# Attention with a gated feed-forward unit: norms in bfloat16, the shift of the scores turned in the bank of the last maxima, tail outputs turned in fp16 parts, and a list schedule that knows when GpSimd holds SBUF

## The chip, the cores and the metric

The kernel runs on one core of a Trainium2 chip. The metric is the device time of an execution in microseconds, given as the median of several runs. The engines are named as in the profile: PE is TensorE's matmuls, PEld its weight loads, DVE is VectorE, ACT is ScalarE, POOL is GpSimd, and SP is the engine that issues all DMAs here.

## The reference

Attention over 8 batches of 8 heads: 576 pooled queries against 1152 keys of 64 dimensions. Its output goes through a feed-forward unit with a gate that mixes the sequence.

```python
q_pool = q.reshape(B, H, S // 2, 2, D).mean(axis=3)
scores = scale * np.matmul(q_pool, k.transpose(0, 1, 3, 2))
scores = scores - np.max(scores, axis=-1, keepdims=True)
attn = np.exp(scores)
attn = attn / (np.sum(attn, axis=-1, keepdims=True) + 1e-09)
x = np.matmul(attn, v)          # heads put side by side: (8, 576, 512)
...
h = np.maximum(x @ w_in, 0.0)   # 512 -> 1024
u, v = h[..., :512], h[..., 512:]
v_n = (v - mean(v)) / np.sqrt(var(v) + 1e-06)
v_s = np.einsum('ts,bsd->btd', w_spatial, v_n) + b_spatial[None, :, None]
out = (u * v_s) @ w_out
```

## The kernel before

All operands are fp32 in memory. Matmuls run in fp16 on parts: a number is scaled by a power of two and written as a head (rounded to fp16) and a rest (what the rounding left), and products are summed over three combinations. `head` is an ACT copy with a scale, `rest` a DVE instruction of three operands, out = in * scale - head, over two tensors that mostly lie in SBUF.

**Attention** goes over 32 pairs of heads. Of the 576 queries of a head, 512 are the main part and 64 the tail; the tails of both heads share tiles. For each pair there are these steps:

- `prep` loads queries and keys, takes their sums of squares on ACT, and calls `scales`: a matmul with a matrix of ones (`ones`, L345) adds a column over all partitions, and three DVE instructions make a power of two from the exponent. This matmul is called the norm. Weights, values and the gated products have norms too. Heads and rests then go to `xq`, `klo` and others.
- `maxima` computes scores roughly, in 27 tiles of 128 queries by 384 keys, each in a PSUM bank (L617 and L608), from which DVE takes the maximum (`mt`, L623). Banks come from a pool of two (`pm`), and from a second pool of two (`pw`) while no unit of the feed-forward part is under way.
- `shift` comes after 15 of the 27 tiles and again at the end. It reduces 5 or 4 columns of maxima (`mx`, L635), turns them on PE by a matmul with the identity into a bank of its own (L639), scales them there, and writes head and rest to `mr` (L642 to L646). Two DMAs bring `mr` into two rows of `xq`, so that the score matmul subtracts the maximum itself.
- `attention` computes scores in two matmuls (L800 and L801, in banks `pss`), exponentials on ACT (L806, into one of eight buffers `pt`), and splits each into two 16-bit halves on POOL (L826). `values` multiplies them with the values (L714, L720, L725) into a bank `o`, of which there is one; when 9 tiles of a head are done, DVE divides (`den`, L693 and L694, then `xm`, L733).
- `tail_values` (L772 to L774) does the same for the tails, and DVE scales its two blocks of 64 by 64 into `xt` (L778). After the fourth pair of a batch, `turn_main` turns the four `xt` on PE by a matmul with `ident2` (L757), and `x_split` makes head (ACT) and rest (DVE) of the result.

**The feed-forward part** runs in four units of two batches each, on PE beside the attention of the following pairs; the last unit runs after the end of attention. It makes the second half of h (L883), its mean and variance, the normalised tiles on DVE (L919 and L925), the first half (L947), the spatial product (L988 and L989), the gated product and its head and rest (L372), and the output (L1031). The three weights are loaded, decoded from 64-bit numbers on DVE and ACT, and split during the first eight pairs.

**The order.** The loops only write down what is to be done. `Order.pin` then lists the instructions: at each step it takes, over all engines, the one that can start first by a table of costs, where on an engine the earliest written of the ready ones goes first, and fixes each engine's order. An engine executes its instructions in that order. The planner keeps `held`, the time for which the last POOL instruction holds the port to SBUF that POOL shares with DVE. A DVE instruction that reads only SBUF (`shared`) and was chosen within that time is put at its end less 130 ns.

Of the kernel before, what the change touches and what calls it, by code (L numbers as in the profile page):

```python
# [31 lines left out]
class Order:  # L32
# [150 lines left out]
    def pin(self, tc):  # L183
# [32 lines left out]
        for _ in prog:  # L216
            best = None
            for e, ns in ready.items():
                if ns:

                    at = {n: max(due[n], wire - 1000) if n in load else due[n] for n in ns}
                    t = max(free[e], min(at.values()))
                    n = min(n for n in ns if at[n] <= t)
                    if best is None or t < best[0]:
                        best = (t, e, n)
# [36 lines left out]
def attn_sgu_kernel(ctx: ExitStack, tc: tile.TileContext, qT, kT, v, w_in, w_spT, b_sp, w_out, out):  # L262
# [41 lines left out]
    ones = const.tile([P, P], F32, name="ones")  # L304
    nc.vector.memset(ones, 1.0)

    ident2 = const.tile([P, D], F32, name="ident2")
# [7 lines left out]
    xt = const.tile([P, NHP, P], F32, name="xt")  # L315
# [24 lines left out]
    def scales(sq, name, up=0):  # L340
# [4 lines left out]
        nc.tensor.matmul(pt[:, :n], lhsT=ones, rhs=sq, start=True, stop=True)  # L345
# [248 lines left out]
    def maxima(i):  # L594
# [5 lines left out]
        for t in range(NT):  # L600
# [25 lines left out]
            if t == 4:  # L626
                yield from shift(st, mt, 0, 5)
        yield
        yield from shift(st, mt, 5, NT)

    def shift(st, mt, a, z):
        X = st["X"]
        n = z - a
        mx = sm.tile([P, NT], F32, name="mx", bufs=2)
        nc.vector.reduce_max(out=mx[:, :n], in_=mt[:, a:z], axis=AX.X)  # L635
        yield
        yield
        pt = ps_m.tile([P, 512], F32, name="pm")
        nc.tensor.transpose(out=pt[:n, :P], in_=mx[:, :n], identity=ident)  # L639
        mr = sm.tile([NT, 2, P], F16, name="mr", bufs=2)  # L640
        m = pt[:n, :P]
        nc.vector.tensor_scalar(  # L642
            out=m, in0=m, scalar1=st["lnp"][:n], scalar2=1.0 / MROW, op0=ALU.subtract, op1=ALU.mult
        )
        nc.vector.tensor_copy(out=mr[:n, 0], in_=m)
        nc.vector.tensor_sub(mr[:n, 1], m, mr[:n, 0])  # L646
        for r in range(2):
            rows = X[D + r : D + r + 1].rearrange("p h s -> p (h s)")
            nc.sync.dma_start(out=rows[:, a * P : z * P], in_=mr[:n, r])
# [90 lines left out]
    def turn_main(i):  # L740
# [13 lines left out]
        if hp == NHP - 1:  # L754
            ps = ps_m.tile([P, 512], F32, name="pm")
            for k in range(NHP):
                nc.tensor.matmul(ps[:, k * D : (k + 1) * D], lhsT=xt[:, k], rhs=ident2, start=True, stop=True)  # L757
            t0 = MAIN + e * TAIL
            x_split(n, slice(0, NHP), slice(t0, t0 + TAIL), ps[:, : NHP * TAIL].rearrange("p (k t) -> p k t", t=TAIL))
# [3 lines left out]
    def tail_values(i):  # L763
# [12 lines left out]
        for h in range(2):  # L776
            rows = slice(h * D, (h + 1) * D)
            nc.vector.tensor_scalar_mul(xt[rows, hp, rows], o[rows, h, 0:D], r[rows])  # L778
# [412 lines left out]
```

## Time and profile before

| | us |
|---|---|
| median of 3 runs | 1218.47 (1217.81 to 1222.07) |
| profiled execution, its time | 1221.1 |
| its span, first to last instruction | 1219.0 |

| stage, us from the start | PE | DVE | ACT | POOL | PE clock |
|---|---|---|---|---|---|
| 0 to 33: first pair's loads and maxima | 11.77 | 20.34 | 16.12 | 7.58 | 0.89 |
| 33 to 290: eight pairs, weights | 215.12 | 231.54 | 197.47 | 218.53 | 0.92 |
| 290 to 1219: 24 pairs, four units | 916.36 | 645.13 | 676.97 | 683.49 | 1.00 |

The second table gives how long each engine was busy. A DVE or POOL instruction that waits for the shared port counts as busy while it waits. Durations of matmuls overlap, since they are pipelined: what one costs PE is the distance from its start to the start of the next.

### The profile page before, as it was taken

What the parts mean: (1) busy time and instruction counts of PE and PEld (TensorE: products, weight loads), DVE (VectorE), ACT (ScalarE), POOL (GpSimd) and SP (SyncE); (2) the same over time, 40 slices, a digit from 0 to 9 for tenths busy, and PEclk for the clock granted to TensorE, in tenths of its full rate; (3) what the DMA queues carried; (4) which work ended last, traced back from release to release, by engine and by line L of the source; (5) the groups of instructions that cost most, each with busy time, mean ns of one, the idle gap of its engine ahead of it and who ended that gap; (6) DMA issues with size and microseconds to landing.
All of it is one profiled execution on the core that took longest, in us unless ns stands there. A gap on an engine that the chain in (4) does not pass through costs nothing.

```text
span 1219.0 us, 34011 instructions
## 1 busy us (share of the span) xinstructions
PE 1143.2 (94%) x13504; PEld 712.6 (58%) x13504; DVE 897.0 (74%) x2163; ACT 890.6 (73%) x1659; POOL 909.6 (75%) x774
## 2 busy tenths in 40 slices
PE   3888888879999999999999999999999999999998
PEld 1555555556666666666666666666665666665453
DVE  5699999997889676865679777865669866841644
ACT  4788778678977887878777887878776786754423
POOL 2769998699888897888787887888887787874000
PEclk9989899899999999999999999999999999999999
DMA  5456464346443553266433443256343421121002
GB/s 189 162 169 169 118 196 120 112 126 169 122 123 95 122 142 105 49 167 179 117 80 99 140 118 89 63 145 196 93 115 98 106 76 47 39 53 45 1 1 78
DMA packets 97151, 135.09 MB, mean 111 GB/s; under 512 B 48544, under 2 KB 56736, under 8 KB 96480
## 3 DMA queue, kind: packets, MB, share of 16 engines
q1 hardware_dynamic: 96992, 132.92, 39.7%
q8 instruction: 106, 1.74, 0.6%
q14 instruction: 53, 0.43, 0.1%
HBM read 81.20 MB, written 9.44 MB: 74 GB/s over the span
## 4 chain that ended last, share of the span: by engine, by line
PE 72%; DVE 16%; ACT 3%; issue 1%; DMA 0%; ACTq 0%; DVEq 0%
PE pss L800 8%; PE pss L801 8%; PE pm L617 7%; PE pw L988 7%; PE pw L883 6%; DVE mt L623 6%; PE pw L1031 5%; PE pw L947 5%; PE o L725 4%; PE o L714 4%; PE o L720 4%; DVE vv L372 2%; PE pss L883 1%; PE pss L988 1%; PE pss L1031 1%
## 5 line engine op out<-in xcount | busy, mean ns | idle before, releaser
L826 POOL TENSOR_TENSOR pt<-pt 128x512 f16<-128x512 f32 x576 | 643.0, 1136 | 154.5 <-ACT pt L806 152.7
L806 ACT ACTIVATE pt<-pss,esc 128x512 f32<-128x512 f32 x576 | 386.7, 686 | 166.3 <-PE pss L801 104.0
L623 DVE TENSOR_REDUCE mt<-pm 128x1 f32<-128x384 f32 x733 | 387.9, 549 | 75.2 <-PE pm L617 66.4
L800 PE MATMUL pss<-qhi,khi 128*128 128x512 f16 x576 | 221.3, 385 | 18.3 <-ACT pt L806 16.9
L801 PE MATMUL pss<-xq,klo 66*128 66x512 f16 x576 | 221.3, 387 | 0.7 <-DMA xq<-mr 0.5
L617 PE MATMUL pm<-khi,qhi 128*128 128x384 f16 x655 | 208.6, 332 | 10.4 <-DVE mt L623 5.2
L714 PE MATMUL o<-vp,pt 128*128 128x65 f16 x2304 | 171.0, 194 | 0.4
L725 PE MATMUL o<-vp,pt 128*128 128x65 f16 x2304 | 169.7, 194 | 0.6 <-POOL pt L826 0.5
L714 PEld LDWEIGHTS <-pt 128*128 128x128 bf16 x2304 | 130.1, 99 | 67.1 <-issue 5.0
L720 PE MATMUL o<-vp,pt 128*128 128x64 f16 x2304 | 168.7, 194 | 0.0
L725 PEld LDWEIGHTS <-pt 128*128 128x128 f16 x2304 | 124.0, 99 | 32.0 <-issue 4.5
L617 PEld LDWEIGHTS <-qhi 128*128 128x128 f16 x768 | 75.3, 100 | 76.5 <-issue 30.2
L720 PEld LDWEIGHTS <-pt 128*128 128x128 bf16 x2304 | 112.2, 99 | 3.3 <-issue 0.3
L883 PE MATMUL pw<-wi_h,xg 128*128 128x512 f16 x240 | 88.4, 378 | 0.0
L801 PEld LDWEIGHTS <-klo 66*128 66x128 f16 x576 | 56.6, 99 | 51.8 <-issue 27.3
L826 POOL TENSOR_TENSOR ptl<-ptl 128x1152 f16<-128x1152 f32 x32 | 74.3, 2321 | 14.4 <-ACT ptl L822 14.4
L947 PE MATMUL pw<-xg,wi_h 128*128 128x512 f16 (+1 forms) x336 | 83.4, 325 | 0.0
L822 ACT ACTIVATE ptl<-pss,esc 128x256 f32<-128x256 f32 (+1 forms) x128 | 63.7, 497 | 26.4 <-PE pss L817 26.2
L988 PE MATMUL pw<-ws_h,vv 128*128 128x512 f16 x216 | 80.6, 379 | 0.0
L1031 PE MATMUL pw<-wo_h,vv 128*128 128x512 f16 x216 | 79.0, 378 | 1.1 <-DVE vv L372 0.9
L623 DVE TENSOR_REDUCE mt<-pw 128x1 f32<-128x384 f32 x131 | 69.6, 543 | 9.3 <-PE pw L617 8.9
L800 PEld LDWEIGHTS <-khi 128*128 128x128 f16 x576 | 57.0, 99 | 26.2 <-issue 6.8
(195 smaller groups left out, 2432.0 us busy)
## 6 DMA issues: line engine op xcount, KB each, us to landing
vt<-in_v_dram SPq DMA_DIRECT2D x56, 576.0 KB
qt<-in_qT_dram SPq DMA_DIRECT2D x32, 576.0 KB
kt<-in_kT_dram SPq DMA_DIRECT2D x32, 576.0 KB
khi<-kn SPq DMA_DIRECT2D x128, 144.0 KB
out_dram<-row SPq DMA_DIRECT2D x24, 256.0 KB
qhi<-xq SPq DMA_DIRECT2D x64, 72.0 KB
klo<-klo SPq DMA_DIRECT2D x32, 144.0 KB
vv<-in_w_in_dram SPq DMA_DIRECT2D x4, 1024.0 KB
```

Source lines behind the costliest of these rows:

```text
L617: nc.tensor.matmul(pm[:, :W], lhsT=qhl[:, h, c0 : c0 + P], rhs=khh[:, h, n * NB : (n + 1) * NB, :], start=True, stop=True,)
L623: nc.vector.reduce_max(out=mt[:, t, n : n + 1], in_=pm[:, :W], axis=AX.X)
L714: nc.tensor.matmul(o[:, t], lhsT=top[:, cols], rhs=vp[:, D : D + D1], start=c == 0 and t == 0, stop=False, skip_group_check=True,)
L720: nc.tensor.matmul(o[:, t, 0:D], lhsT=top[:, cols], rhs=vp[:, 0:D], start=False, stop=False, skip_group_check=True)
L725: nc.tensor.matmul(o[:, t], lhsT=rst[:, cols], rhs=vp[:, D : D + D1], start=False, stop=c == NC - 1, skip_group_check=True,)
L800: nc.tensor.matmul(o, lhsT=khh[:, h, c, :], rhs=qhl[:, h, q], start=True, stop=False)
L801: nc.tensor.matmul(o, lhsT=KL[0:KR, h, c, :], rhs=X[0:KR, h, q], start=False, stop=True)
L806: nc.scalar.activation(pt, ps, AF.Exp, bias=0.0, scale=esc)
L826: nc.gpsimd.tensor_sub(t.bitcast(F16)[..., 0::2], t, t.bitcast(BF16)[..., 1::2])
L883: nc.tensor.matmul(ph, lhsT=xa[:, cc, c0 : c0 + P], rhs=wa[:, cc, DH:DF], start=n == 0, stop=n == 3 * NCC - 1,)
L988: nc.tensor.matmul(pv, lhsT=l, rhs=r[:, 0:MAIN], **fl)
L1031: nc.tensor.matmul(py, lhsT=ga[:, fc, c0 : c0 + P], rhs=wa[:, fc, :], start=m == 0, stop=m == end - 1)
```

## The change

1. **Norms.** `ones` becomes bfloat16, and the sums enter by the upper 16 bits of each fp32 number. A norm is one bfloat16 matmul instead of fp32.
2. **Shift.** The reduced maxima no longer go to SBUF, but into free columns of the bank that held the last tile of maxima (`pm` or `pw`). They are scaled there, and head and rest go to one tile `mc` side by side. One fp16 transpose with a new fp16 identity turns both, into the end of the same bank, and one DVE copy takes them to `mr`. No other bank is taken. The DMAs are the same in number and size.
3. **Tail outputs.** `tail_values` writes head (ACT) and rest (DVE) in fp16 to `xt`, which is doubled. `turn_main` turns the eight parts with an fp16 `ident2`, and one ACT copy takes them; `x_split` is no longer called there.
4. **List schedule.** Where DVE chooses its next instruction, one that reads only SBUF and could start only while POOL holds the port counts as ready at the end of that time less 130 ns. Another instruction can so be chosen ahead of it. Before, it was chosen and then put there.

```diff
@@ Order.pin
                     at = {n: max(due[n], wire - 1000) if n in load else due[n] for n in ns}
+                    if e == "DVE":
+                        for n in ns:
+                            if shared[n] and max(free[e], at[n]) >= held[0]:
+                                at[n] = max(at[n], held[1] - 130)
                     t = max(free[e], min(at.values()))
...
-    ones = const.tile([P, P], F32, name="ones")
+    ident_h = const.tile([P, P], F16, name="ident_h")
+    nc.vector.tensor_copy(out=ident_h, in_=ident)
+    ones = const.tile([P, P], BF16, name="ones")
...
-    ident2 = const.tile([P, D], F32, name="ident2")
+    ident2 = const.tile([P, D], F16, name="ident2")
...
-    xt = const.tile([P, NHP, P], F32, name="xt")
+    xt = const.tile([P, 2, NHP, P], F16, name="xt")
@@ scales
-        nc.tensor.matmul(pt[:, :n], lhsT=ones, rhs=sq, start=True, stop=True)
+        nc.tensor.matmul(pt[:, :n], lhsT=ones, rhs=sq.bitcast(BF16)[:, 1::2], start=True, stop=True)
@@ shift
-        mx = sm.tile([P, NT], F32, name="mx", bufs=2)
-        nc.vector.reduce_max(out=mx[:, :n], in_=mt[:, a:z], axis=AX.X)
-        yield
-        yield
-        pt = ps_m.tile([P, 512], F32, name="pm")
-        nc.tensor.transpose(out=pt[:n, :P], in_=mx[:, :n], identity=ident)
-        mr = sm.tile([NT, 2, P], F16, name="mr", bufs=2)
-        m = pt[:n, :P]
-        nc.vector.tensor_scalar(
-            out=m, in0=m, scalar1=st["lnp"][:n], scalar2=1.0 / MROW, op0=ALU.subtract, op1=ALU.mult
-        )
-        nc.vector.tensor_copy(out=mr[:n, 0], in_=m)
-        nc.vector.tensor_sub(mr[:n, 1], m, mr[:n, 0])
+        m = pm[:, KEYS // 3 : KEYS // 3 + n]
+        nc.vector.reduce_max(out=m, in_=mt[:, a:z], axis=AX.X)
+        nc.vector.tensor_scalar(out=m, in0=m, scalar1=st["lnp"], scalar2=1.0 / MROW, op0=ALU.subtract, op1=ALU.mult)
+        mc = sm.tile([P, 2 * NT], F16, name="mc", bufs=2)
+        nc.vector.tensor_copy(out=mc[:, 0:n], in_=m)
+        nc.vector.tensor_sub(mc[:, n : 2 * n], m, mc[:, 0:n])
+        yield
+        yield
+        t = pm.bitcast(F16)[: 2 * n, 2 * (512 - P // 2) :]
+        nc.tensor.transpose(out=t, in_=mc[:, : 2 * n], identity=ident_h)
+        mr = sm.tile([2 * NT, P], F16, name="mr", bufs=2)
+        nc.vector.tensor_copy(out=mr[: 2 * n], in_=t)
@@ turn_main
-            for k in range(NHP):
-                nc.tensor.matmul(ps[:, k * D : (k + 1) * D], lhsT=xt[:, k], rhs=ident2, start=True, stop=True)
+            pz = ps.rearrange("p (l k t) -> p l k t", l=2, t=D)
+            for l in range(2):
+                for k in range(NHP):
+                    nc.tensor.matmul(pz[:, l, k], lhsT=xt[:, l, k], rhs=ident2, start=True, stop=True)
             t0 = MAIN + e * TAIL
-            x_split(n, slice(0, NHP), slice(t0, t0 + TAIL), ps[:, : NHP * TAIL].rearrange("p (k t) -> p k t", t=TAIL))
+            nc.scalar.activation(x_parts(n)[:, :, :, t0 : t0 + TAIL], pz, AF.Copy, bias=0.0, scale=1.0)
@@ tail_values
-            nc.vector.tensor_scalar_mul(xt[rows, hp, rows], o[rows, h, 0:D], r[rows])
+            hd = xt[rows, 0, hp, rows]
+            nc.scalar.activation(hd, o[rows, h, 0:D], AF.Copy, bias=0.0, scale=r[rows])
+            rest(xt[rows, 1, hp, rows], o[rows, h, 0:D], r[rows], hd)
```

The change adds ten lines, so the line numbers after it are up to ten higher (L623 becomes L629, L372 becomes L378, L733 becomes L739, L919 becomes L929, L925 becomes L935). It also moves instructions. Three places follow, all on DVE.

The first is the first shift, some 24 us from the start. Before, the rows are the last maxima of the first half (L623), the reduction to `mx` (L635), then other work, and the three instructions on the turned maxima (L642, L645, L646):

```order
L623 TENSOR_REDUCE mt<-pw 128x1 x2
L635 TENSOR_REDUCE mx<-mt 128x5
L623 TENSOR_REDUCE mt<-pw 128x1 x5
L361 TENSOR_REDUCE vt<-vsq 128x1
L350 TENSOR_SCALAR pm<-pm 128x1
L642 TENSOR_SCALAR pm<-pm,lnp 5x128
L355 TENSOR_SCALAR vr<-pm 128x1
L356 TENSOR_SCALAR vs<-pm 128x1
L645 CAST mr<-pm 5x128
L646 TENSOR_TENSOR mr<-pm,mr 5x128
```
After, the reduction goes into the bank (L642), and scaling, head and rest (L643 to L646) and the copy of the turned tile (L652) follow it:

```order
L629 TENSOR_REDUCE mt<-pw 128x1 x2
L642 TENSOR_REDUCE pw<-mt 128x5
L643 TENSOR_SCALAR pw<-pw,lnp 128x5
L645 CAST mc<-pw 128x5
L646 TENSOR_TENSOR mc<-pw,mc 128x5
L652 COPY mr<-pw 10x128
L629 TENSOR_REDUCE mt<-pw 128x1 x2
L367 TENSOR_REDUCE vt<-vsq 128x1
L629 TENSOR_REDUCE mt<-pw 128x1
L356 TENSOR_SCALAR pm<-pm 128x1
```
The whole shift now stands ahead of the sum and the scales of the values (`vt`; then `vr` and `vs`).

The second place is some 152 us from the start, where the first head of a pair ends. The rest of the next keys (`klo`) is a `shared` instruction; `den` and `xm` empty the bank `o`. Before:

```order
L372 SCALAR_TENSOR_TENSOR klo_106<-kt,qks,kn 128x640
L693 TENSOR_SCALAR dent<-pm 128x1
L623 TENSOR_REDUCE mt<-pm 128x1
L694 RECIPROCAL dent<-dent 128x1
L693 TENSOR_SCALAR den<-o 128x4
L623 TENSOR_REDUCE mt<-pw 128x1
L778 TENSOR_SCALAR xt<-pm,dent 64x64 x2
L694 RECIPROCAL den<-den 128x4
L623 TENSOR_REDUCE mt<-pw 128x1
L733 TENSOR_TENSOR xm<-o,den 128x4x64
```
After:

```order
L378 SCALAR_TENSOR_TENSOR qhi_120<-qt,qks,xq_114 128x576
L699 TENSOR_SCALAR dent<-pm 128x1
L699 TENSOR_SCALAR den<-o 128x4
L629 TENSOR_REDUCE mt<-pw 128x1
L700 RECIPROCAL dent<-dent 128x1
L700 RECIPROCAL den<-den 128x4
L629 TENSOR_REDUCE mt<-pw 128x1
L739 TENSOR_TENSOR xm<-o,den 128x4x64
L378 SCALAR_TENSOR_TENSOR xt<-pm,dent,xt 64x64 x2
L367 TENSOR_REDUCE vt<-vsq 128x1
```
The rest of the keys is no longer ahead of `den` and `xm`; it stands 16 rows behind `xm`. The rests of the tail outputs (`xt`) have moved behind `xm` too.

The third place is the beginning of the first unit's normalised tiles, behind the last step of the inverse root (`rs`). Before, with `row` the difference times `rs` and `vv` the rest:

```order
L915 TENSOR_TENSOR rs<-rs,pm 128x9
L919 TENSOR_SCALAR row<-vv,mv,rs 128x512
L623 TENSOR_REDUCE mt<-pm 128x1 x2
L693 TENSOR_SCALAR den<-o 128x4
L623 TENSOR_REDUCE mt<-pm 128x1
L694 RECIPROCAL den<-den 128x4
L623 TENSOR_REDUCE mt<-pm 128x1
L733 TENSOR_TENSOR xm<-o,den 128x4x64
L925 TENSOR_TENSOR vv<-row,vv 128x512
```
After:

```order
L925 TENSOR_TENSOR rs<-rs,pm 128x9
L700 RECIPROCAL den<-den 128x4
L739 TENSOR_TENSOR xm<-o,den 128x4x64
L629 TENSOR_REDUCE mt<-pm 128x1 x10
L929 TENSOR_SCALAR row<-vv,mv,rs 128x512 x2
L629 TENSOR_REDUCE mt<-pm 128x1
L356 TENSOR_SCALAR pm<-pm 128x2
L361 TENSOR_SCALAR qkr<-pm 128x2
L362 TENSOR_SCALAR qks<-pm 128x2
L935 TENSOR_TENSOR vv<-row,vv 128x512 x2
```
Ten reductions of maxima stand ahead of the first tile, and the tiles then go two by two.

More of the change, by code (lines that the diff above doesn't have):

```diff
@@ L626, in maxima, with shift @@
             if t == 4:
-                yield from shift(st, mt, 0, 5)
+                yield from shift(st, mt, pm, 0, 5)
         yield
-        yield from shift(st, mt, 5, NT)
-    def shift(st, mt, a, z):
+        yield from shift(st, mt, pm, 5, NT)
+    def shift(st, mt, pm, a, z):
         X = st["X"]
         n = z - a
-        mx = sm.tile([P, NT], F32, name="mx", bufs=2)
-        nc.vector.reduce_max(out=mx[:, :n], in_=mt[:, a:z], axis=AX.X)
+        m = pm[:, KEYS // 3 : KEYS // 3 + n]
[4 more added lines that the diff above has]
+        nc.vector.tensor_sub(mc[:, n : 2 * n], m, mc[:, 0:n])
         yield
         yield
-        pt = ps_m.tile([P, 512], F32, name="pm")
-        nc.tensor.transpose(out=pt[:n, :P], in_=mx[:, :n], identity=ident)
-        mr = sm.tile([NT, 2, P], F16, name="mr", bufs=2)
-        m = pt[:n, :P]
-        nc.vector.tensor_scalar(
-            out=m, in0=m, scalar1=st["lnp"][:n], scalar2=1.0 / MROW, op0=ALU.subtract, op1=ALU.mult
-        )
-        nc.vector.tensor_copy(out=mr[:n, 0], in_=m)
-        nc.vector.tensor_sub(mr[:n, 1], m, mr[:n, 0])
+        t = pm.bitcast(F16)[: 2 * n, 2 * (512 - P // 2) :]
+        nc.tensor.transpose(out=t, in_=mc[:, : 2 * n], identity=ident_h)
+        mr = sm.tile([2 * NT, P], F16, name="mr", bufs=2)
+        nc.vector.tensor_copy(out=mr[: 2 * n], in_=t)
         for r in range(2):
             rows = X[D + r : D + r + 1].rearrange("p h s -> p (h s)")
-            nc.sync.dma_start(out=rows[:, a * P : z * P], in_=mr[:n, r])
+            nc.sync.dma_start(out=rows[:, a * P : z * P], in_=mr[r * n : (r + 1) * n])
         yield
```

## The prediction

> **What bounds the kernel now.** I read the page's busy shares, then the busy time by stages, cut where TensorE's load changes, then who waits for whom in each stage.
>
> ```profile
> span 1219.0 us, 34011 instructions
> PE 1143.2 (94%) x13504; PEld 712.6 (58%) x13504; DVE 897.0 (74%) x2163; ACT 890.6 (73%) x1659; POOL 909.6 (75%) x774
> ```
> ```profile
> 0.00:33.00 33.00, 11.77 (x40) 4.65 (x41) 20.34 (x47) 16.12 (x33) 7.58 (x16) 0.89 0.53 175
> 33.00:290.00 257.00, 215.12 (x2795) 140.09 (x2794) 231.54 (x501) 197.47 (x360) 218.53 (x166) 0.92 0.52 147
> 290.00:1219.00 929.00, 916.36 (x10672) 567.88 (x10672) 645.13 (x1617) 676.97 (x1267) 683.49 (x593) 1.00 0.37 98
> ```
> The columns are PE, PEld, DVE, ACT, POOL, the granted clock, and DMA. From 290 us on TensorE is busy in 916 of 929 us at full clock, and no other engine exceeds 683. So there the price of an instruction is its distance to the next start on TensorE, and work on the other engines is hidden. Before 290 us it is different: TensorE has 42 us idle, and DVE (231 of 257) and POOL (218) carry the stage. Their busy figures hold waiting:
>
> ```profile
> L826 POOL TENSOR_TENSOR pt<-pt x576: 1032/1043/2273, 33.4 to 1114.4; 128x512 f16<-128x512 f32 x192
> L826 POOL TENSOR_TENSOR pt<-pt 128x512 f16<-128x512 f32 x144 | 180.0, 1281 | 36.4 <-ACT pt L806 36.4
> L925 DVE TENSOR_TENSOR vv<-row,vv x36: 649/692/1794, 360.9 to 1158.0; 128x512 f16<-128x512 f32 x36
> ```
> The first and third are min/median/max in ns; the second is the stage from 33 to 290 us. A split on POOL takes 1.04 us, but 1.28 in the mean there: 144 x 0.24 = 34 us in which POOL stands behind a DVE instruction. The same DVE subtraction takes 0.69 or up to 1.79 us: there DVE stands behind POOL. Both read two operands from SBUF.
>
> **TensorE's part.** Removed are fp32 matmuls: norms (L345), transposes of the maxima (L639), turns of the tail outputs (L757). Their number from 290 us on, as (x) in the busy time of each line alone, in that order:
>
> ```profile
> 290.00:1219.00 929.00, 10.15 (x66) 10.73 (x66) 1.00 0.37 98
> 290.00:1219.00 929.00, 12.51 (x46) 4.16 (x46) 1.00 0.37 98
> 290.00:1219.00 929.00, 7.26 (x56) 6.84 (x56) 1.00 0.37 98
> ```
> A norm's fp32 matmul runs as two, a transpose as one, and the four matmuls of a turn as eight, so these are 33 norms, 46 transposes and 7 turns. What each occupies is read from the timeline, from its start to the next line's:
>
> ```profile
> 606.93 0.28 PE L345 MATMUL pm<-sq,ones 128*128 128x2 f32 x2
> 607.07 0.28 PE L714 MATMUL o<-vp,pt 128*128 128x65 f16 x4
> 607.18 0.28 PE L720 MATMUL o<-vp,pt 128*128 128x64 f16 x4
> ...
> 715.71 0.36 PE L345 MATMUL pm<-sq,ones 128*128 128x2 f32 x2
> 715.93 0.19 PE L725 MATMUL o<-vp,pt 128*128 128x65 f16 x1
> ...
> 592.20 0.27 PE L639 MATMUL pm<-ident,mx 128*4 128x128 f32 x1
> 592.31 0.38 PE L800 MATMUL pss<-qhi,khi 128*128 128x512 f16 x1
> ...
> 709.45 1.02 PE L757 MATMUL pm<-ident,xt 128*128 128x64 f32 x8
> 710.30 0.33 PE L617 MATMUL pm<-khi,qhi 128*128 128x384 f16 x1
> ...
> 448.90 0.22 PE L773 MATMUL pm<-vp,ptl 128*128 128x128 f16 x1
> 448.96 0.22 PE L774 MATMUL pm<-vp,ptl 128*128 128x130 f16 x1
> ```
> ```profile
> L720 PEld LDWEIGHTS <-pt 128*128 128x128 bf16 x2304 | 112.2, 99 | 3.3 <-issue 0.3
> ```
> - Norm: 0.14 us behind a long matmul (607.07 - 606.93), 0.22 behind short ones; I take 0.17. As one bfloat16 matmul of two columns it is nearest to L714, four of which take 0.11 us, so 0.03 each though each has a weight load of 0.10 (L720 on PEld: loads run ahead). Saved: 33 x 0.14 = 4.6 us. Ends: 33 x (0.14 - 0.10) = 1.3, were its load in the open each time; 33 x 0.19 = 6.3.
> - Transpose: 0.11 us. In fp16, again 128 moving columns, it is nearest to L773, 0.06. Saved: 46 x 0.05 = 2.3 us; ends 0 and 2.8.
> - Turn: 0.85 us for eight. Now again eight pieces (four pairs x two fp16 parts) of 64 columns at 0.03: 0.24. Saved: 7 x 0.61 = 4.3 us; ends 1.4 (0.65 for the eight) and 4.3.
>
> Together 11.2 us (2.7 to 13.4). The Trainium skill speaks against this on "TensorE: Matmul & The Clock Gate", section "Back-to-back issue gap": in a real stream of weight loads and matmuls it gives a sustained 81 ns a matmul at 128 columns, so the eight pieces would take an estimated 0.65 us and a transpose 0.08, and the sum would be 7.4 us instead of 11.2. The trace disagrees, with 0.06 us at 128 columns and 0.03 at 65, each with a load of its own.
>
> **The other engines, from 290 us on.** Rows of the groups by line (count | busy us, mean ns):
>
> ```profile
> L635 DVE TENSOR_REDUCE mx<-mt 128x5 f32<-128x15 f32 x32 | 5.3, 164 | 0.3
> L642 DVE TENSOR_SCALAR pm<-pm,lnp 5x128 f32<-5x128 f32 x32 | 11.0, 344 | 24.2 <-PE pm L639 24.0
> L645 DVE CAST mr<-pm 5x128 f16<-5x128 f32 x32 | 8.7, 273 | 0.2
> L778 DVE TENSOR_SCALAR xt<-pm,dent 64x64 f32<-64x64 f32 x64 | 18.0, 282 | 1.0
> L957 ACT ACTIVATE u<-pw,r_h 128x64 f32<-128x64 f32 x28 | 7.2, 314 | 0.0
> ```
> A shift on DVE is now 0.16 + 0.34 + 0.27 + 0.27 = 1.05 us. Afterwards it is a reduction, three instructions over 4 or 5 columns (0.16 each, like L635) and one copy of 128 columns (0.16 to 0.27): 0.8 to 0.9, or 64 x 0.2 = 13 us less DVE work. Tail outputs: 64 ACT heads at 0.31 (like L957) are 20 us more on ACT, and the 64 DVE remainders cost what L778 does. The last copy on ACT doubles its columns, and DVE's subtraction behind it goes. ACT would come to some 75%: hidden behind TensorE; were TensorE to run out, some 14 us (46 of the 64 heads, after 290 us) would show. The DMAs stay in number.
>
> New waits: DVE's copy of the turned shift waits for TensorE, with reductions queued behind it; ACT's heads wait for DVE's reciprocal, with exponentials queued. The shift now holds the last maxima bank through four DVE steps, the transpose and the copy (about 1.4 us more), but takes no second bank, which was held 1.2. I take zero for these, since TensorE's waits after 290 us are a few us in all; ends -2 and +6.
>
> **The list's part, before 290 us.** One place, with POOL holding SBUF:
>
> ```profile
> 152.67 0.98 DVE L372 SCALAR_TENSOR_TENSOR klo<-kt,qks,kn 128x640 f16<-128x640 f32 x1
> 155.62 0.42 DVE L733 TENSOR_TENSOR xm<-o,den 128x256 f32<-128x256 f32 x1
> 156.72 1.84 ACT L806 ACTIVATE pt<-pss,esc 128x512 f32<-128x512 f32 x3 [2.73 <-PE o L725]
> 157.49 3.49 POOL L826 TENSOR_TENSOR pt<-pt 128x512 f16<-128x512 f32 x2 [2.94 <-ACT pt L806]
> ```
> ```profile
> POOL pt L826 <- ACT pt L806: 36.4, 13, 10.2
> ACT pt L806 <- PE o L725: 31.8, 15, 5.8
> ```
> The split of the keys (L372) stands ahead of the chain that frees the output bank (den, xm). While DVE waits there, the bank comes late, L725 and so the pt buffers come late, ACT idles 2.73 us and POOL 2.94. The two sums say that this kind of wait costs POOL 36 us and ACT 32 in the stage. In the new order the split stands behind xm at this place. What can come back at most is POOL's idle 38 us; but a DVE split that runs later still blocks POOL for its whole 0.7 to 0.9 us, so POOL's 34 us of standing stay. Most of the long waits have several causes (the longest, 10.2, is pair 1's first scores waiting for maxima and shift), so I take some two waits of the kind above, 5 us; ends -4 (a split that is now late for its pair) and 15.
>
> **Start-up.** The first shift's DMA:
>
> ```profile
> 24.46 0.16 DVE L635 TENSOR_REDUCE mx<-mt 128x5 f32<-128x15 f32 x1
> 27.76 0.37 PE L639 MATMUL pm<-ident,mx 128*5 128x128 f32 x1
> 28.86 10.19 SPq L649 DMA_DIRECT2D xq<-mr  x4
> 32.68 0.69 ACT L806 ACTIVATE pt<-pss,esc 128x512 f32<-128x512 f32 x1
> ```
> The maxima were ready at 24.6, but the transpose stood behind the values' norm on TensorE. In the new order it stands ahead of it, and its DMA goes some 3 us sooner. ACT has four splits of the values before the first exponential, so I count 0.8 us (0 to 2). The new fp16 identity costs DVE about 1 us ahead of its first norm, where it sat idle for 4.54 us:
>
> ```profile
> 8.63 0.17 DVE L350 TENSOR_SCALAR pm<-pm 128x2 int32<-128x2 int32 x1 [4.54 <-PE pm L345]
> ```
>
> **The sum.** 11.2 + 0 + 5 + 0.8 = 17 us. The profiled execution took 1221.1 us, 0.2% over the median of 1218.47; I take the 17 us off the median: 1201.5, say 1202.
>
> **Rivals.**
> 1. TensorE's savings come, the list's don't: the stage before 290 us is set by the exclusive use of SBUF, where order only changes who stands. For it: DVE and POOL stand for one another in both directions. Then 1218.5 - 11.2 = 1207; with norms and transposes at their low ends, 1212. The Trainium skill, "SBUF — State Buffer", section "SBUF: two separate sides", has a lock held for the whole instruction, the loser blocked fully, and that is this rival's mechanism; the long forms of L826 and L925 agree.
> 2. Nothing measurable: TensorE's shorter list turns into waits of the same size, because the shift keeps one of two maxima banks longer (1.4 us against 1.2 for a bank of its own). It decides from 0.24 us a shift on (46 x 0.24 = 11); with nothing from the list either, 1218. Against it: TensorE has scores, values and the second half's matmuls to take meanwhile, and waits little now.
> 3. Slower: DVE's two-operand instructions are put off again and again. POOL is busy 683 of 929 us, the planner passes over such an instruction whenever POOL would hold it, and in the new order ten reductions go ahead of the first normalised tile of a unit (third place of the order). One hold costs up to 1.1 us (L925, 1.79 - 0.69), nine tiles a unit 10 us; were 6 of them in the open in each of four units, 24 - 17 = +7, so 1225. It decides from 4.3 us a unit on. Against it: a unit's last tile stands only some five places later, and TensorE's waits for DVE in all that stretch are these:
>
> ```profile
> PE pm L617 <- DVE mt L623: 2.0, 7, 0.6
> ```
> The others are smaller.
>
> **How the numbers follow.** Half a per cent, 6 us, is about what can be told from no change. My case 0.58; rival 1 0.22 (mostly still faster); rival 2 0.11; rival 3 0.09. Of my case nearly all and of rival 1 nine tenths are faster: 0.78. Same: 0.14. Slower: 0.08. The likeliest case alone runs from 1193 to 1208. The range reaches to rival 1's low end, and below to the upper ends of list and start-up together (11 + 15 + 2 = 28): 1190 to 1213.
>
> **What the new profile would show.** Norms, transposes and turns at 0.03, 0.06 and 0.24 us from start to start, and the stretch with TensorE above 98% shorter by about 11 us. DVE's two-operand instructions at lengths nearer their minima, and POOL's 36 us of waits for ACT in the first stage smaller, with unit 0's first matmul some 6 us earlier. I would be wrong if L617 came to wait for the bank of the shift, if L1031 or L988 waited for DVE, or if the first stage ended where it does now.

## The result and the profile after

The changed kernel takes 1258.81 us (median of 4 runs, 1256.79 to 1259.78) against 1219.55: a ratio of 1.032, with a 95% interval from 1.029 to 1.034. It is slower by 39 us, where 17 us less were forecast. Two of the eleven executions of one experiment below (the turn as a matmul) took 2327 and 2966 us, and its ratio goes by the other nine. The profiled execution took 1259.78 us. The first lines of its page, then the chain of waits of before and of after, as shares by engine:

```profile
span 1258.0 us, 33964 instructions
PE 1151.2 (92%) x13456; PEld 701.5 (56%) x13456; DVE 912.0 (72%) x2220; ACT 913.1 (73%) x1723; POOL 912.1 (73%) x774
```
```profile
PE 72%; DVE 16%; ACT 3%; issue 1%; DMA 0%; ACTq 0%; DVEq 0%
```
```profile
PE 66%; DVE 24%; ACT 2%; issue 2%; DMA 0%; SPq 0%; POOL 0%; DVEq 0%; ACTq 0%; POOLq 0%
```
No engine has become much busier. What grew is the share of the path that runs over DVE, from 16 to 24%. To compare equal work, both runs are cut where ACT starts the first exponential of the tenth pair and of the last pair. The columns are PE, PEld, DVE, ACT, POOL, clock, DMA; the first two stages, before first:

```profile
0.00:318.00 318.00, 254.88 (x3175) 162.75 (x3176) 272.53 (x599) 238.29 (x443) 250.87 (x204) 0.92 0.54 154
318.00:1085.20 767.20, 758.87 (x9337) 482.24 (x9336) 571.27 (x1435) 596.98 (x1118) 635.52 (x550) 1.00 0.40 106
```
```profile
0.00:331.60 331.60, 257.00 (x3162) 160.51 (x3163) 284.14 (x625) 244.82 (x458) 253.15 (x204) 0.89 0.50 146
331.60:1125.60 794.00, 765.68 (x9304) 474.33 (x9302) 575.01 (x1466) 612.33 (x1165) 635.66 (x550) 1.00 0.37 104
```
The first stage costs 13.6 us more. The long one costs 26.8 us more, though PE executes the same matmuls in it (fewer records, as a norm's fp32 matmul counted as two): there PE is busy 96.4% instead of 98.9% of the time. The end takes 132.4 us, 1.4 less. So what I had called hidden behind TensorE is not hidden: of the 26.8 us, 20.0 are idle time of PE (28.3 us instead of 8.3), and 6.8 are PE being busy longer. Some of PE's and PEld's waits for DVE over the whole run, in before and after (total, times, longest, us); a load and its matmul can wait at the same moment, so the rows don't add up to lost time:

```profile
PEld pm L639 <- DVE mx L635: 5.2, 10, 1.6
PEld L617 <- DVE xt L778: 6.2, 10, 2.0
PE pm L617 <- DVE mt L623: 5.2, 11, 1.4
PE pm L617 <- DVE xt L778: 1.1, 2, 0.5
```
```profile
PEld L650 <- DVE mc L646: 21.2, 22, 2.9
PEld L623 <- DVE xt L378: 16.9, 26, 3.0
PE pm L623 <- DVE mt L629: 20.0, 34, 4.0
PE pm L623 <- DVE xt L378: 7.9, 10, 2.7
```
Three places stand out: the turn of the shift waits for `mc`, the maxima for the tail's rests (`xt`, whose bank they take next), and the maxima for the reductions (`mt`) that empty their banks. In the long stage alone, the last of these was 2.0 us before (quoted in the prediction) and is now:

```profile
PE pm L623 <- DVE mt L629: 12.4, 26, 2.1
```
The experiments take the parts in turn. They ran on several chips, on which the kernel before took 1221.48 to 1223.52 us, so kernels are compared by the ratio to the kernel before on the same chip, given with its 95% interval.

### The profile page after: what moved, and what is told of

It reads as the page before. It is cut to its first block, busy times and chain, and to the rows that moved or that the text cites. A ratio compares the mean times of both kernels' runs of the same rounds, so it can differ in the third digit from the quotient of the medians.

```text
span 1258.0 us, 33964 instructions
## 1 busy us (share of the span) xinstructions
PE 1151.2 (92%) x13456; PEld 701.5 (56%) x13456; DVE 912.0 (72%) x2220; ACT 913.1 (73%) x1723; POOL 912.1 (73%) x774
## 4 chain that ended last, share of the span: by engine, by line
PE 66%; DVE 24%; ACT 2%; issue 2%; DMA 0%; SPq 0%; POOL 0%; DVEq 0%; ACTq 0%; POOLq 0%
DVE mt L629 7%; PE pss L810 7%; PE pm L623 7%; PE pss L811 7%; PE pw L998 6%; PE pw L893 6%; PE pw L1041 5%; PE o L720 4%; PE o L731 4%; PE o L726 4%; PE pw L957 4%; DVE vv L378 2%; PE pss L893 1%; PE pss L998 1%; DVE row L929 1%
## 5 line engine op out<-in xcount | busy, mean ns | idle before, releaser
L816 ACT ACTIVATE pt<-pss,esc 128x512 f32<-128x512 f32 x576 | 387.2, 685 | 118.3 <-PE pss L811 98.9
L629 DVE TENSOR_REDUCE mt<-pm 128x1 f32<-128x384 f32 x733 | 388.7, 550 | 105.3 <-PE pm L623 91.0
L623 PE MATMUL pm<-khi,qhi 128*128 128x384 f16 x655 | 213.2, 335 | 31.8 <-DVE mt L629 20.0
L810 PE MATMUL pss<-qhi,khi 128*128 128x512 f16 x576 | 223.9, 389 | 9.6 <-ACT pt L816 9.3
L811 PE MATMUL pss<-xq,klo 66*128 66x512 f16 x576 | 224.2, 390 | 0.0
L623 PEld LDWEIGHTS <-qhi 128*128 128x128 f16 x768 | 74.1, 100 | 85.5 <-issue 35.0
L1041 PE MATMUL pw<-wo_h,vv 128*128 128x512 f16 x216 | 80.1, 380 | 5.1 <-DVE vv L378 5.1
L957 PE MATMUL pw<-xg,wi_h 128*128 128x512 f16 (+1 forms) x336 | 80.7, 325 | 0.0
L629 DVE TENSOR_REDUCE mt<-pw 128x1 f32<-128x384 f32 x131 | 69.2, 545 | 8.9 <-PE pw L623 8.0
```

The costliest lines, as they stand in the source:

```text
L623: nc.tensor.matmul(pm[:, :W], lhsT=qhl[:, h, c0 : c0 + P], rhs=khh[:, h, n * NB : (n + 1) * NB, :], start=True, stop=True,)
L629: nc.vector.reduce_max(out=mt[:, t, n : n + 1], in_=pm[:, :W], axis=AX.X)
L810: nc.tensor.matmul(o, lhsT=khh[:, h, c, :], rhs=qhl[:, h, q], start=True, stop=False)
L811: nc.tensor.matmul(o, lhsT=KL[0:KR, h, c, :], rhs=X[0:KR, h, q], start=False, stop=True)
L816: nc.scalar.activation(pt, ps, AF.Exp, bias=0.0, scale=esc)
L1041: nc.tensor.matmul(py, lhsT=ga[:, fc, c0 : c0 + P], rhs=wa[:, fc, :], start=m == 0, stop=m == end - 1)
```

## The experiments

### The parts alone

Each part was put alone into the kernel before; the diffs are those of the change, cut at its four numbers. A last kernel has all but the list.

> The kernel before with the norms in bfloat16 alone. Two theories of the 39 us that the whole change costs: W (waits): the new chains of the shift and of the tail outputs pass through more steps ahead of a TensorE instruction that stands in order, and TensorE waits for them; O (order): the list that heeds GpSimd's hold is to blame. Both expect the same here: TensorE saves 48 norms of 0.11 to 0.14 us, 5 to 6 us, so 1213 us; a result above 1219 would say that any new order costs time.

> The kernel before with the new shift alone (norms, tail outputs and list as before). W: the transpose now waits behind four short instructions of VectorE instead of one; after the whole change TensorE and its weight loads waited 33 us for the last of them (mc), against 7 us for mx before, so +12 to +25 us: 1231 to 1244. O: VectorE has 13 us less to do, 1215 to 1219.

> The kernel before with the tail outputs in fp16 parts alone. W: a tail's bank is now held through head (ACT), rest (VectorE), head, rest, one after the other; after the whole change TensorE's maxima waited 25 us for these rests, against 7 us for the two scalings before, so +10 to +18 us: 1229 to 1237. O: the turns save TensorE 4 us and the rest is hidden, 1214 to 1218.

> The kernel before with the hold-heeding list alone: the same instructions in another order. W: within 5 us of before, 1214 to 1224. O: most of the 39 us, 1245 to 1260.

> The whole change without the list's part: norms, shift and tail outputs in the new form, planned as before. If the parts add up (0 or -1, +7 and +7 us in the first runs): 1231 to 1238; if they make one another worse, above 1242; if the new order of the list is all that matters, 1220 to 1226.

| kernel | median us | ratio (interval) | to the tenth pair | to the last pair | the end |
|---|---|---|---|---|---|
| before (as in the result) | 1219.55 | 1 | 318.0 | 767.2 | 133.8 |
| norms | 1221.99 | 0.999 (0.996 to 1.002) | 318.4 | 765.0 | 133.8 |
| shift | 1231.37 | 1.006 (1.003 to 1.009) | 334.8 | 769.6 | 133.7 |
| tail | 1229.46 | 1.005 (1.004 to 1.007) | 323.2 | 770.8 | 133.2 |
| list | 1241.29 | 1.015 (1.011 to 1.018) | 324.2 | 782.2 | 133.4 |
| all but the list | 1233.17 | 1.009 (1.006 to 1.012) | 321.3 | 775.8 | 132.4 |
| the whole change | 1258.81 | 1.032 (1.029 to 1.034) | 331.6 | 794.0 | 132.4 |

The last three columns are the stages of the profiled execution, cut as above; the shift's has 8 us in its first stage from one long stand, shown at the end. Neither theory holds alone. The list is the largest single part, 18 us, but only half of the loss; shift and tail lose 7 us each, as the theory of waits said, at the low end or under its ranges. The norms' 6 us did not show (the kernel before took 1223.34 us on that chip). Without the list the parts add up; the list on top of them costs 28 us more by the ratios (1.032 against 1.009), not 18.

A control tells what another order, made for no purpose, is worth:

```diff
-t = max(t, held[1] - 130)
+t = max(t, held[1] - 120)
```


> A control: the kernel before, with 120 instead of 130 ns in the planner's rule for the port. The same instructions, and the order moves in many places by chance. It tells what a mere reshuffling of this list is worth: within 4 us of before (1217 to 1226) if the parts' differences are their own; more than 6 us off if any new order can cost what the shift and the tail part cost.

1220.63 us, ratio 0.998 (0.996 to 1.001). This other order costs nothing. It is one order and a mild one: counted by names without buffer numbers, 86 of DVE's 2163 places hold another instruction, with the list alone 795. A kernel further down (the late unbunched list) changes 764 places and loses 4.0 us in the long stage, against the list's 15.0, so the number of moved instructions alone does not set the cost either.

### The turn of the shift

```diff
-t = pm.bitcast(F16)[: 2 * n, 2 * (512 - P // 2) :]
-nc.tensor.transpose(out=t, in_=mc[:, : 2 * n], identity=ident_h)
+t = pm[: 2 * n, KEYS // 3 :]
+nc.tensor.matmul(t, lhsT=mc[:, : 2 * n], rhs=ident_h, start=True, stop=True)
```


> The new shift alone, its turn as a plain matmul into fp32 columns of the same bank instead of a transpose into fp16 ones. In the run of the shift alone a turn took TensorE 0.15 us from start to start, where before it was 0.11 and where I had counted 0.06. Theory P (the turn's own time): the plain matmul takes 0.06, 64 x 0.09 = 6 us less, some 4 to 6 of them on the path: 1225 to 1227. Theory W (waits for the longer chain of VectorE): the time stays, 1229 to 1233.

1230.57 us, ratio 1.006 (1.004 to 1.008), and the turn still took 0.15 us. That looked like the theory of waits, but it only says that a transpose and a matmul of this shape cost the same. The shape itself was the next thing to change: `mc` became one of two tiles of 128 columns, zero beyond the 8 or 10 that are used.

```diff
-mc = sm.tile([P, 2 * NT], F16, name="mc", bufs=2)
+mc = mcs[a > 0]          # two [P, P] fp16 tiles, set to zero once
-t = pm[: 2 * n, KEYS // 3 :]
-nc.tensor.matmul(t, lhsT=mc[:, : 2 * n], rhs=ident_h, start=True, stop=True)
+t = pm[:, KEYS // 3 :]
+nc.tensor.matmul(t, lhsT=mc, rhs=ident_h, start=True, stop=True)
```


> The new shift alone, its turn as a matmul over 128 columns (the head and rest in a tile of 128 columns, the others zero) instead of 8 or 10. In the run with the plain matmul the turn took 0.15 us as the transpose did; around it the load of its 8 or 10 columns starts 0.12 us behind the matmul ahead of it and the next load 0.15 us behind its own, where elsewhere loads run ahead. Theory P: the narrow 16-bit load is not run ahead, and with 128 columns the turn takes 0.06 us and the matmul ahead of it 0.03: 64 x 0.2 = 13 us less on TensorE, 46 x 0.2 = 9 of them in the long stage: 1220 to 1224. Theory W (waits for VectorE's four steps set the cost): 1228 to 1233.

1218.97 us, ratio 0.996 (0.993 to 0.998): the shift now gains 5 us instead of losing 7. The same place in three kernels, a turn between four value matmuls and a score matmul, PE first and then PEld: before (the turn and the score matmul on PE are quoted in the prediction, at 592.20 and 592.31), the whole change, the wide turn:

```profile
592.08 0.29 PE L725 MATMUL o<-vp,pt 128*128 128x65 f16 x4
...
592.17 0.08 PEld L639 LDWEIGHTS pm<-ident,mx 128*4 128x4 f32 x1
592.20 0.10 PEld L800 LDWEIGHTS <-khi 128*128 128x128 f16 x1
```
```profile
748.05 0.29 PE L731 MATMUL o<-vp,pt 128*128 128x65 f16 x4
748.26 0.22 PE L650 MATMUL pm<-ident_h,mc 128*10 128x128 f16 x1
748.42 0.39 PE L810 MATMUL pss<-qhi,khi 128*128 128x512 f16 x1
...
748.26 0.08 PEld L650 LDWEIGHTS <-mc 128*10 128x10 f16 x1
748.41 0.10 PEld L810 LDWEIGHTS <-khi 128*128 128x128 f16 x1
```
```profile
754.14 0.29 PE L730 MATMUL o<-vp,pt 128*128 128x65 f16 x4
754.26 0.22 PE L649 MATMUL pm<-ident_h,mca 128*128 128x128 f16 x1
754.32 0.38 PE L805 MATMUL pss<-qhi,khi 128*128 128x512 f16 x1
...
754.24 0.10 PEld L649 LDWEIGHTS <-mca 128*128 128x128 f16 x1
754.27 0.10 PEld L805 LDWEIGHTS <-khi 128*128 128x128 f16 x1
```
The narrow fp16 load starts only with its matmul (748.26), 0.09 us after its turn would have come, and the next load starts 0.15 us later: loads run ahead on neither side. Over 128 columns, and before in fp32 over 4, they do. From the start of the four value matmuls to the score matmul it is 0.37 us narrow (748.42 - 748.05), 0.18 wide, and 0.23 before (592.31 - 592.08). It is not this place alone: over the 55 turns of each run ahead of which and behind which PE does not wait, the median from the turn to the next start is 0.15 us with the narrow transpose and 0.06 with the wide matmul. Narrow against wide that is 64 x 0.19 = 12 us, about what the time fell by; 44 of the turns are in the long stage, 8.4 us, and that stage took 769.6 us with the narrow transpose, 770.4 with the narrow matmul and 763.2 with the wide one.

The waits for `mc` did not go with it. What PE and PEld waited ahead of the turn (total, times), with the narrow transpose and with the wide matmul:

```profile
DVE mc L642: 18.1, 26
```
```profile
DVE mca L645: 13.4, 17
DVE mcb L645: 5.8, 11
```
That is 18.1 and 19.2 us (before, for `mx`: 7.4), and the wide one is faster than before all the same. So these waits are not what made the shift slower.

Is it the small number of columns that keeps the loads from running ahead, or any number short of 128? Nothing but the number differs here from the wide turn:

```diff
-nc.tensor.matmul(t, lhsT=mc, rhs=ident_h, start=True, stop=True)
+nc.tensor.matmul(t, lhsT=mc[:, :64], rhs=ident_h, start=True, stop=True)     # t: 64 rows
```


> As the wide turn, but over 64 columns of the tile. One look: from the matmul ahead of the turn to the turn, and from the turn to the next matmul. If only a full load of 128 columns runs ahead, 0.12 and 0.15 us as with 8 or 10 columns, and a time like that of the shift alone; if it is the small number that matters, 0.03 and 0.06 us.

```profile
764.68 0.29 PE L730 MATMUL o<-vp,pt 128*128 128x65 f16 x4
764.90 0.24 PE L649 MATMUL pm<-ident_h,mca 128*64 128x128 f16 x1
765.07 0.39 PE L805 MATMUL pss<-qhi,khi 128*128 128x512 f16 x1
```
With 64 columns it is 0.39 us, and one run took 1230.71 us, as with 8 and 10: each width tried short of 128 does it. The Trainium skill has a rule on this, on "TensorE: Matmul & The Clock Gate", section "Weight-path perf modes — Fast Weight Load (FWL) and DoubleRow": the fast load is on where there are 128 weights and the type is not FP32. The trace agrees for the three widths in fp16; but by that rule the fp32 turn of before had no fast load either, and its load ran ahead, so the rule alone does not explain the rows.

The wide turn in the whole change:

> The whole change with the one edit of the wide turn. Theory P (the narrow turn's own time on TensorE): the 12 us that the wide turn gave to the shift alone come back here too, 1259 - 12 = 1247, 1244 to 1250. If the waits for the shift's VectorE steps set the cost in the whole change, less than 4 us come back: 1255 to 1260.

1251.36 us, ratio 1.024 (1.021 to 1.027): 7 to 9 us come back, between the two forecasts and nearer to the turn's own time. In the long stage PE is busy for 757.5 us instead of 765.7 (before: 758.9), and idle about as long, 29.3 us instead of 28.3. So the turn was the busy part of the loss; the idle part has other causes: without the list it is 14.1 us (all but the list, 775.8 - 761.7).

### The list

What does the new order do on DVE? A place in the list's run, where the rests of the first unit's gated products (`vv`) are written; DVE, then POOL, then PE's two waits:

```profile
513.10 3.95 DVE L376 SCALAR_TENSOR_TENSOR vv<-u,gs,vv 128x576 f16<-128x576 f32 x3
516.97 1.52 DVE L627 TENSOR_REDUCE mt<-pm 128x1 f32<-128x384 f32 x3
...
513.42 1.38 POOL L830 TENSOR_TENSOR pt<-pt 128x512 f16<-128x512 f32 x1 [0.74 <-ACT pt L810]
514.76 1.67 POOL L751 TENSOR_TENSOR xc<-xm,xc 128x512 f16<-128x512 f32 x1
516.39 1.56 POOL L830 TENSOR_TENSOR pt<-pt 128x512 f16<-128x512 f32 x1
...
515.47 0.82 PE L1035 MATMUL pw<-wo_h,vv 128*128 128x512 f16 x3 [0.55 <-DVE vv L376]
517.57 0.32 PE L621 MATMUL pm<-khi,qhi 128*128 128x384 f16 x1 [0.84 <-DVE mt L627]
```
Three rests in a row take 3.95 us (0.80, 1.59 and 1.71), since GpSimd takes the port between them. PE waits first for a rest and then, two banks full, for the reductions behind the row. The rule makes such rows: all instructions that were put off until a hold's end become ready at the same moment. Counted in the traces (DVE instructions of 256 elements or more that read SBUF only, from 300 us to the last pair's first exponential), 7 of 117 stand second or later in a row before, 40 of 118 with the list alone, 44 of 120 after the whole change. A rule that breaks the rows up:

```diff
                             if shared[n] and max(free[e], at[n]) >= held[0]:
                                 at[n] = max(at[n], held[1] - 130)
+                            if shared[n]:
+                                at[n] = max(at[n], dve + 1050)
```


> The list of the change alone, with one rule more: behind a VectorE instruction that reads only SBUF the planner lets the next such one count as ready 1050 ns later, the length of one GpSimd split, so that other work is put between. Theory B (bunching): put off until the hold ends, such instructions become ready together, go out in a row, and the second one stands behind GpSimd's next split; in the list alone 74 of 198 long ones are second or later in a row (before: 19 of 197), and TensorE waits for the reductions behind the row. B expects most of the list's 18 us back: 1220 to 1228. Theory D (delay): it is the putting off itself, work that comes late for TensorE; putting off still more should cost as much or more, 1240 to 1255.

1271.37 us, ratio 1.041 (1.038 to 1.044): slower still, as the theory of delay said. But its stages are 365.5, 768.4 and 138.0: all of its loss lies ahead of the tenth pair and in the end, and the long stage is within 1.2 us of before, as the theory of bunching said. So the two were separated by place: both edits only where the planner's time is past 300 us, and then the list's rule alone there.

```diff
-if shared[n] and max(free[e], at[n]) >= held[0]:
+if shared[n] and max(free[e], at[n]) >= held[0] and free[e] > 300000:
...
-if shared[n]:
+if shared[n] and free[e] > 300000:     # the second kernel leaves this rule out
```


> The list's part with the rule of the run 'unbunched', but both only where the planner's time is past 300 us; up to there the list is that of before. In the profiles, by the first exponential of the tenth pair and from there to that of the last pair: before 318.0 and 767.2 us; the list alone 324.2 and 782.2; unbunched 365.5 and 768.4. Theory S (by stage): in the long stage the bunching alone costs the list's 15 us, and the unbunched list's 50 us arise in the first stage alone, where VectorE is the bound and each further delay counts; then this run is within 4 us of before, 1217 to 1225. If putting off costs in the long stage too, 1230 or more.

> The list's part only where the planner's time is past 300 us, without the rule that unbunches; the partner of the run 'late unbunched' (1231.7 us, of which 4 arose in the last 134 us, where GpSimd has no work and the added rule only delays). Bunching: the long stage costs its 15 us, 1234 to 1240, and VectorE's rows of two or more are back there. If the list's cost comes from the first stage and what it hands on, 1221 to 1228.

The long stage of the late list (rule alone), and of the late unbunched one:

```profile
331.00:1114.90 783.90, 762.64 (x9337) 482.28 (x9336) 575.64 (x1435) 600.68 (x1118) 635.13 (x550) 1.00 0.38 104
```
```profile
321.20:1092.40 771.20, 761.17 (x9337) 481.74 (x9336) 578.10 (x1435) 596.38 (x1117) 641.45 (x550) 1.00 0.39 106
```
Same instructions, nearly the same busy times; 16.7 us over before with the rule alone (42 of 118 in rows) and 4.0 us with rows broken up (11 of 118). PE's waits for the reductions in the long stage go the same way, late list first:

```profile
PE pm L621 <- DVE mt L627: 7.0, 14, 1.1
```
```profile
PE pm L623 <- DVE mt L629: 3.4, 9, 0.8
```
and its waits for `vv` fall from 3.3 to 0.6 us. Three quarters of the list's cost in the long stage go with the rows. The stages are those of one execution each, and the late list's, at 1250.12 us, was the slowest of six; the first list's run, near its median, has 15.0 us in this stage. In whole times the late list took 1242.43 us, 1.015 (1.010 to 1.020), over its forecast, and the late unbunched one 1231.71, 1.006 (1.004 to 1.008). That is outside the forecast of theory S and, by the time alone, in that of its rival; but 4.3 us of its loss are in the end, where GpSimd is busy for only 23 us and my added rule delays without need.

Two things stay open. What the rule costs ahead of the tenth pair (6 us in the list's own run) was not taken apart: bunching and delay are both there. And in the whole change with the wide turn the list costs more than alone, 18.2 us in the long stage (786.8 against 768.6 without it, with 44 and 9 instructions in rows) and 7.9 ahead of it; why more was not tested.

### The tail

Theory: the tail's bank is held longer. Two kernels free it earlier, by a copy of the scaled blocks to SBUF, on VectorE and on ACT; a third keeps the bank and makes the heads on VectorE.

```diff
+xf = sm.tile([P, D], F32, name="xf", bufs=2)
+for h in range(2):        # on VectorE; or nc.scalar.activation(xf[rows], ..., scale=r[rows])
+    nc.vector.tensor_scalar_mul(xf[rows], o[rows, h, 0:D], r[rows])
 for h in range(2):
     hd = xt[rows, 0, hp, rows]
-    nc.scalar.activation(hd, o[rows, h, 0:D], AF.Copy, bias=0.0, scale=r[rows])
-    rest(xt[rows, 1, hp, rows], o[rows, h, 0:D], r[rows], hd)
+    nc.scalar.activation(hd, xf[rows], AF.Copy, bias=0.0, scale=1.0)
+    nc.vector.tensor_sub(xt[rows, 1, hp, rows], xf[rows], hd)
```
```diff
-nc.scalar.activation(hd, o[rows, h, 0:D], AF.Copy, bias=0.0, scale=r[rows])
+nc.vector.tensor_scalar_mul(hd, o[rows, h, 0:D], r[rows])
```


> The tail outputs in fp16 parts alone, but VectorE first scales both blocks from the bank into SBUF, as before the change, and head and rest are taken from there; 64 VectorE instructions more. Theory H (hold): the tail's bank is held longer by the chain head, rest, head, rest, and TensorE's maxima wait for it; then the bank is free as early as before, and the time comes to 1216 to 1222 in spite of the added work. Theory C (the added work on ACT and VectorE costs): as slow as with the tail part alone or slower, 1229 to 1235.

> The tail outputs in fp16 parts, scaled from the bank into SBUF by ACT (64 more ACT instructions), heads and rests taken from SBUF; VectorE has the 64 rests as in the tail part alone, not the 64 more of the run 'tail copy', which took 16 us more than the tail part alone. Theory H (hold of the bank): the bank is free after two ACT instructions, 1217 to 1224. Theory V (VectorE's work counts, not the bank): no better than the tail part alone, 1227 to 1235.

> The tail outputs in fp16 parts alone, heads on VectorE instead of ACT, still read from the bank. In the two runs with a copy in SBUF the rests of 0.2 us, reading SBUF only, took up to 1.24 us behind GpSimd, so these did not test the hold of the bank; here nothing reads SBUF only. Theory H (the chain head, rest, head, rest with its two crossings each and ACT's queue holds the bank): on one engine it is shorter, and TensorE's waits for it (23 us with the tail part alone) fall; 1220 to 1226. Theory V (each added VectorE instruction delays the maxima behind it): 64 x 0.28 = 18 us more VectorE work, 1230 to 1240.

They took 1245.63, 1240.36 and 1236.40 us: 1.020 (1.017 to 1.023), 1.013 (1.009 to 1.016) and 1.011 (1.008 to 1.015), all slower than the tail part alone (1.005). The copies brought a cost of their own. The rests of the second one, min/median/max in ns:

```profile
L786 DVE TENSOR_TENSOR xt<-xf,xt x64: 205/322/1415, 69.4 to 1125.1; 64x64 f16<-64x64 f32 x64
```
Work of 0.2 us takes up to 1.4, because it now reads SBUF alone and stands behind GpSimd. So these two say nothing on the bank. PE's waits for the tail's rests with the tail part alone, and with heads on VectorE:

```profile
PEld L617 <- DVE xt L372: 17.7, 29, 3.8
PE pm L617 <- DVE xt L372: 5.9, 9, 2.1
```
```profile
PEld L617 <- DVE xt L372: 11.6, 20, 3.8
PE pm L617 <- DVE xt L372: 3.3, 1, 3.3
```
The waits for the bank are there (23.6 us, loads and matmuls added, against 7.3 before) and fall to 14.9, yet the time rises by 7 us, as theory V said: 64 x 0.28 = 18 us of added VectorE work cost more than the shorter hold gave. That the hold makes the tail's 7 us is argued from these waits, not shown: no kernel here shortened it without adding work.

### The good parts together, and what is left

Norms and the wide turn, without tail and list; then the whole change with the wide turn but without the list.

> Norms in bfloat16 and the new shift with the turn over 128 columns; tail outputs and list as before. If the parts add up (-0.1% and -0.4% in the runs of each alone): 1213 to 1219, faster than before by 0.3 to 0.7%. If VectorE's waits eat what TensorE saves, 1219 to 1224.

> The whole change without the list's part and with the wide turn. With norms and wide turn alone 1213.6 us, with the list as well 1251.4. If the tail part costs here what it costs alone (7 us): 1218 to 1223, and the list in this company costs 28 to 33 us; if the tail part and the list divide the 38 us otherwise, 1226 or more.

| kernel | median us | ratio (interval) |
|---|---|---|
| norms and wide turn | 1213.62 | 0.993 (0.990 to 0.997) |
| and the tail part | 1224.18 | 1.000 (0.998 to 1.002) |
| and the list (whole change, wide turn) | 1251.36 | 1.024 (1.021 to 1.027) |
| and the narrow turn (whole change) | 1258.81 | 1.032 (1.029 to 1.034) |

The first is faster than both kernels, by 8 us over before; its long stage takes 762.7 us instead of 767.2. Read downwards, in steps of the ratio, the 39 us are -8 for norms and wide turn, +8 for the tail part, +30 for the list, and +9 for the narrow turn, each uncertain by 4 to 5 us.

## Why the prediction was wrong

Forecast and measurement are 56 us apart. By the steps above about 35 of them lie in the list (-5 forecast, +30 measured), 12 in the tail outputs (-4.3 and +8), and 9 in the narrow turn; norms, wide turn and start-up together came as forecast (-7.7 and -8).

- **Norms: right in size, little of it in the time.** After, a norm among value matmuls takes 0.03 us (707.34 - 707.31), as taken:

```profile
707.31 0.16 PE L351 MATMUL pm<-sq,ones 128*128 128x2 bf16 x1
707.34 0.25 PE L726 MATMUL o<-vp,pt 128*128 128x64 f16 x3
```
  Alone the part gave 2.2 us in the long stage against the 4.6 forecast, and in the time no difference that can be told.
- **Turns of the tail outputs: right.** Eight pieces take 0.23 us to the next start (forecast 0.24):

```profile
1155.46 0.40 PE L765 MATMUL pm<-ident,xt 128*128 128x64 f16 x8
1155.69 0.38 PE L1041 MATMUL pw<-wo_h,vv 128*128 128x512 f16 x1
```
  The 0.65 us that I had estimated by the Trainium skill ("TensorE: Matmul & The Clock Gate", section "Back-to-back issue gap") did not come here.
- **Transposes: the mis-sized term.** I took 0.06 us by "again 128 moving columns, it is nearest to L773" and gave 0 as the low end. L773 has 128 columns of weights, the turn 8 or 10. It took 0.15 us, and 0.09 more ahead of it: 0.14 us more than before instead of 0.05 less. The nearest row has to be near in the weights too; with 128 columns the 0.06 came out (754.32 - 754.26).
- **DVE, ACT, POOL from 290 us on, 0 (-2 to +6): the step that failed.** It went by busy shares ("hidden behind TensorE"). But PE takes the maxima in order with two banks, and as I read the waits, a DVE instruction ahead of a reduction delays PE as soon as PE's order has nothing else in between: PE's waits for `mt` in the long stage went from 2.0 to 12.4 us, and 18 us of VectorE work added to the tail came with 7 us more time. The "New waits", taken at zero, named the shift's copy and ACT's heads, and not the waits that came: PE behind the reductions, behind the tail's rests, and behind `mc`, of which the last did not make the shift slower. Of the signs that I had named, L1031 (now L1041) came to wait for DVE, 5.1 us instead of 0.9, and the first stage ended later; L617 (now L623) hardly waits for the shift's bank, 0.6 us in the long stage.
- **The list, 5 us (-4 to 15): wrong in sign.** I read a gain from one place in the first stage and did not ask what an instruction that is put off meets at the hold's end. Rival 3 had the mechanism's trigger, the putting off, and the third place of the order showed "the tiles then go two by two"; I priced it by single stands (1.1 us each), at +7 us and 0.09. In the long stage most of the price is in the row: the second stand, and the reductions that wait behind both.
- **Start-up, 0.8 us: right.** The shift's DMA is issued 3.0 us sooner (25.90 instead of 28.86 us), as read, and the first exponential starts at 31.67 instead of 32.68 us.
- **Rivals 1 and 2** did not come: the list did not merely give nothing, and the bank held by the shift is no loss as such, since the shift with the wide turn holds it too and gains.

## What to carry to other kernels

An engine at 99% busy is not a cover for the others when it executes in a fixed order: ask for each instruction added or put off elsewhere which of its next instructions waits behind it, and how many banks lie between. Putting off work until a shared port is free gathers it at that moment, and the second in the row meets the port taken again. Breaking up the rows took most of that cost away in the long stage, but here every list with instructions put off was slower than letting the first one stand. When a matmul is made cheaper by type, compare its weights as well as its moving columns with the row that gives the price, and try them filled up to 128 if they are fewer; here that was worth 9 to 12 us.

## What the runs showed of the hardware

- An fp16 load of 8, 10 or 64 columns was not run ahead of its matmul, nor was the load behind it: 0.37 and 0.39 us from the value matmuls to the score matmul, against 0.18 with 128 columns.
- VectorE does not get the port in turn with GpSimd each time. In the shift's profiled run the first of these two splits of 128x1024 took 7.57 us: it stood through six GpSimd instructions that followed one another without a gap, and ended 1.1 us after the last of them (DVE, then POOL):

```profile
292.57 8.76 DVE L374 SCALAR_TENSOR_TENSOR wo_l<-u,wos,wo_h 128x1024 f16<-128x1024 f32 x2
...
292.66 4.05 POOL L828 TENSOR_TENSOR pt<-pt 128x512 f16<-128x512 f32 x4
296.66 1.40 POOL L544 TENSOR_TENSOR qt<-qt 128x576 f32<-128x576 f32 x1
298.01 1.05 POOL L828 TENSOR_TENSOR pt<-pt 128x512 f16<-128x512 f32 x1
```
  PE then waited 6.05 us. In the late list's profiled run the same split took 8.94 us. The longest VectorE instruction of the profiled run was 2.7 us before and 3.4 us after the change. Runs of one kernel may differ by several us for this alone; that was not tried.
